# Sparse attention and a Fourier mixing block on one core: the first attention in program order without weight conversion beside it, one mask pattern, block sums by pair, and seven products for eight in half of the first second layer

## The chip, the cores and the metric

The kernel runs on one core of a Trainium2 chip. The metric is the device time of one execution in microseconds (us). Five engines work side by side: TensorE (PE in the profile; its weight loads are PEld), VectorE (DVE), ScalarE (ACT), GpSimd (POOL) and SyncE (SP), which here only issues DMAs. SBUF holds tiles of 128 partitions, PSUM holds what TensorE sums up.

## What is computed

The reference has two parts, all in f32.

```python
# attention: q, k, v are (4, 8, 768, 64)
k_sum = k.reshape(B, H, nb, block, D).max(axis=3)      # block = 32, nb = 24
v_sum = v.reshape(B, H, nb, block, D).mean(axis=3)
mask_l = np.abs(pos[:, None] - pos[None, :]) < window  # window = 16
scores_all = concat([where(mask_l, scale * q @ k.T, -1e9), scale * q @ k_sum.T + log(block)])
attn = softmax(scores_all) @ concat([v, v_sum])
# mixing: x is attn as (4, 768, 512); w_ch1 (512, 2048) and w_ch2 (2048, 512) are float64
u = x + real(fft(fft(x, axis=1), axis=2))
un = (u - mean(u)) / sqrt(var(u) + 1e-6)
out = u + max(un @ w_ch1, 0) @ w_ch2
```

Each query thus sees the keys at a distance under 16 and one summary of each block of 32 keys: the maximum of the keys, the mean of the values, with 32 in the weight. The batch has four images.

## The kernel before, in words

All the work is in `_main_program`. The four images pass one after another through attention, a Fourier stage, a first layer (512 to 2048) and a second layer (2048 to 512), the two layers in two halves c = 0, 1 of eight blocks j of hidden columns: `gen_hidden(b, 0)`, `gen_out(b, 0)`, `gen_hidden(b, 1)`, `gen_out(b, 1)`. Attention of image b + 1 is mixed into the layers of image b, and the last `gen_out` of an image is mixed with the Fourier stage of the next one.

**First attention (image 0).** Heads are taken in four pairs g. `load` fetches q and k of a pair (`qn`, `kn`, 384 KB each). `prepare` (L656) transposes them by products with the identity (L668), ScalarE copies them into `qt` and `kt` (L670), and VectorE takes the maxima of blocks (`km`, L679). `wide_scores` (L685) goes over 12 windows of 64 queries and 96 keys (L695), with 32 rows more for the block maxima (L699); ScalarE takes the exponential (L701) and VectorE multiplies by the mask `wide`, one pattern of 64 columns for each of the 12 windows, because the first and last window have keys outside the sequence. `wide_values` (L713) multiplies by the values `vw` (L718), whose 65th column holds `count` and so gives the divisor, and VectorE divides (L723 and a multiplication). `block_sums` (L584) fetches the values once more, for two pairs together (four loads `vb`, 96 rows of 512), and adds them up on GpSimd (L563), for image 1 on VectorE (L560 and L605). `sum_values` (L705) picks a pair's sums by a product with `sel` (L709) and ScalarE spreads them into rows 96 to 128 of `vw` (L710). Images 1 to 3 use narrower windows (`scores`, `sum_scores`, `values`).

**Weights.** `w_ch1` and `w_ch2` arrive as 64-bit words. `convert` (L847) turns half a block into f32: four VectorE operations of 128x512 (L857, L858, L862, L864), two on ScalarE (L859, L860) and a multiplication. `make` (L870) does so for both halves of a block, forms the sums that the seven products of W1 need, and stores the block to DRAM (`dw1`, `dw2`) for the later images. `plan` (L827) lists the blocks with the stage that must have been issued before each: `(1, 0, None)` is W1's first block, done during the first attention, `(1, 1, ("fold", 0))` the second, after the fold of image 0. For image 1 `get_w2` (L915) fetches four parts of a W2 block, forms the other three (`_right_sums`, four VectorE subtractions of 128x256), and stores them.

**Fourier stage.** `gen_fourier` (L972) folds `x` on VectorE (sums and differences of halves, with three small copies in each of two rounds), TensorE multiplies by tables along the sequence (`y`, L1014) and along the columns (`mx`, L1040 for image 0, L963 later), VectorE adds and normalizes, TensorE transposes (`unt`, L1079). `keep_busy` (L952) issues products without use while image 0 is folded.

**Layers.** `gen_hidden` (L1086) forms each 2x2 of blocks by seven products for eight (L1101); ScalarE and VectorE combine them (L1111 and after). `gen_out` (L1133) is plain for image 0: 6 row tiles, 4 blocks, 2 halves, each product with 512 columns (L1142), then one addition to `x` for each tile. For later images it takes three pairs of row tiles, and in each seven products, summed over four blocks, of 256 columns (L1167); four left sums of 128x512 go before, and seven additions of 128x256 to `x` come after.

**Order.** SP issues the DMAs of `fetch` in program order up to the layers of image 0, over eight DMA semaphores in rotation, so that a DMA waits for the landing of the eighth before it. The other engines are ordered by the scheduler of the Tile framework, by its own estimate of times and by priorities (`drive`, L1243, raises them for the first of its generators). PSUM has four buffers for attention (`abank`) and four for the rest (`bank`).

Of the kernel before, what the change touches and what calls it, by code (L numbers as in the profile page):

```python
# [16 lines left out]
P = 128  # L17
# [405 lines left out]
def _tables(S, DM):  # L423

    g = _general_consts(S, DM)
    nb = S // BLOCK

    r, i, c = np.arange(96)[:, None, None], np.arange(S // QB)[None, :, None], np.arange(QB)[None, None, :]
    tok = QB * i - W + r
    wide = np.ones((P, S // QB, QB), dtype=np.float32)  # L430
    wide[0:96] = (r > c) & (r < c + 2 * W) & (tok >= 0) & (tok < S)
    count = np.zeros((P, 1), dtype=np.float32)
    count[0:96], count[96:96 + nb] = 1.0, BLOCK

    r, i, c = np.arange(64)[:, None, None], np.arange(nb)[None, :, None], np.arange(BLOCK)[None, None, :]
    tok = BLOCK * i - W + r
    near = (r > c) & (r < c + 2 * W) & (tok >= 0) & (tok < S)
    near = np.concatenate([near, near]).astype(np.float32)


    sel = np.zeros((4 * nb, 2, 2, 2, 32), dtype=np.float32)
    half = np.zeros((2, 2, 32, 2), dtype=np.float32)
    for h in range(2):
        half[:, h, :nb, h] = 1.0
        for e in range(2):
            for pair in range(2):
                for n in range(nb):
                    sel[(2 * pair + e) * nb + n, pair, e ^ h, h, n] = 1.0

    fs = np.ascontiguousarray(np.moveaxis(g["fs"], 2, 0))  # L450


    fd = g["fd"].reshape(P, 6, DM // 2)
    n = DM // 4
    odd = fd[:, 1, 1:n].copy()
    odd[0] = 0.0
    fm = np.concatenate([fd[:, 0, 0:n + 1], fd[:, 3, 0:n], odd, fd[:, 4, 0:n], fd[:, 1, 0:n + 1]], axis=1)
    fm = np.ascontiguousarray(fm)
    return dict(wide=wide, near=near, sel=sel.reshape(4 * nb, 2, P), half=half.reshape(P, 2), count=count, fs=fs,
                fd=g["fd"], fm=fm, ident=g["ident"])  # L460
# [26 lines left out]
def _main_program(ctx, tc, q, k, v, moe_w_ch1, moe_w_ch2, out):  # L487
# [36 lines left out]
    wide = bpool.tile([P, NC, 2, S], FP, tag="h", name="wide").rearrange("p j h s -> p (j h s)")  # L524
    wide = wide[:, 0:NQ * QB].rearrange("p (n c) -> p n c", n=NQ)
    near = cpool.tile([P, 2, NB2, BLOCK], FP, name="near")
    sel = cpool.tile([4 * nb, 2, P], FP, name="sel")
    half_of = cpool.tile([P, 2], FP, name="half")
    count = cpool.tile([P, 1], FP, name="count")
    rebias = cpool.tile([P, 1], FP, name="rebias")  # L530
# [52 lines left out]

    def block_sums(b, gg):  # L584

        f = BLOCK // 4
        n = f * D
        if done_weights:
            raw = room(f"vb_{b}_{gg}")
            raw = [raw[0:4 * nb, n * i:n * (i + 1)] for i in range(4)]  # L590
        else:

            raw = [bpool.tile([P, NC, P], FP, tag="s", bufs=5, name=f"vb_{b}_{gg}_{i}").rearrange("p n t -> p (n t)")
                   [0:4 * nb] for i in range(4)]
        for i in range(4):
            fetch(out=raw[i], in_=v[b, 4 * gg:4 * gg + 4].rearrange("h (n f) d -> (h n) (f d)", f=BLOCK)
                  [:, n * i:n * (i + 1)])
        vb = spool.tile([4 * nb, D], FP, tag="vbs", bufs=2, name=f"vbs_{b}_{gg}")

        add = tt if b == 1 else gtt  # L600
        add(raw[0], raw[0], raw[1], ADD)
        add(raw[2], raw[2], raw[3], ADD)
        add(raw[0], raw[0], raw[2], ADD)
        if b == 1:
            nc.vector.tensor_reduce(out=vb, in_=raw[0].rearrange("p (f d) -> p d f", d=D), op=ADD, axis=AX.X)  # L605
        else:
            while f > 2:
                f //= 2
                gtt(raw[0][:, 0:f * D], raw[0][:, 0:f * D], raw[0][:, f * D:2 * f * D], ADD)
            gtt(vb, raw[0][:, 0:D], raw[0][:, D:2 * D], ADD)  # L610
        sums[b, gg] = vb

# [7 lines left out]
    def load_values(b, g):  # L620
        if g % 2 and following(b, g, 1):
            block_sums(*divmod((b * NP + g + 1) // 2, NP // 2))
        (load_wide_values if is_wide(b) else load_narrow_values)(b, g)

    def load_wide_values(b, g):

        vw = wide_vw(g)
        for e in range(2):
            off = v[b, 2 * g + e].offset
            parts = [(W, WK, 0, NQ), (0, W, 1, NQ)] if (b, g, e) == (0, 0, 0) else [(0, WK, 0, NQ)]  # L630
            for r0, r1, i0, i1 in parts:
# [4 lines left out]
    def load_narrow_values(b, g):  # L636
# [3 lines left out]
        if g < 2 and is_wide(b - 1):  # L640
            nc.gpsimd.memset(vw[WK:P, :, D:D1], 1.0)
        for e in range(2):
# [12 lines left out]

    def prepare(b, g):  # L656
        qn, kn = nat[b, g]
        kt, km = kt_bufs[g % 2], km_bufs[g % 2]
        qt = apool.tile([P, S], FP, tag="qt", name=f"qt_{b}_{g}")
        for src, dst in ((kn, kt[:, W:W + S]), (qn, qt)):  # L660
            if is_wide(b):
                for j0, j1 in ((0, 2), (2, 3)):
# [22 lines left out]
    def wide_scores(b, g):  # L685
# [3 lines left out]
        for half in range(2):  # L689
# [10 lines left out]
            for e in range(2):  # L700
                nc.scalar.activation(out=p[:, e, n0:n1], in_=ps[e], func=AF.Exp, scale=SC)  # L701
                tt(p[:, e, n0:n1], p[:, e, n0:n1], wide[:, n0:n1], ALU.mult)
        return p

    def sum_values(b, g):  # L705

        ps = abank([P, 2, D], f"vs_{b}_{g}")
        for e in range(2):
            nc.tensor.matmul(ps[WK:P, e], sel[:, g % 2, D * e:D * e + 32], sums[b, g // 2], start=True, stop=True)  # L709
        nc.scalar.copy(out=wide_vw(g)[WK:P, :, :, 0:D],  # L710
# [43 lines left out]
    def values(b, g, p, pm, x):  # L754
        vw = vw_bufs[g % 2]
        ps = abank([P, D], f"vs_{b}_{g}")
        nc.tensor.matmul(ps, sel[:, g % 2, :], sums[b, g // 2], start=True, stop=True)
        tt(vs[:, :, 0:D], ps[:, None, :].to_broadcast([P, 2, D]),
# [29 lines left out]
    def gen_attention(b):  # L788
        x = bpool.tile([P, NST, DM], FP, tag="x", bufs=2, name=f"x_{b}")
        x_of[b] = x  # L790
        for g in range(NP):
            p = (wide_scores if is_wide(b) else scores)(b, g)
            yield
            if is_wide(b):
                sum_values(b, g)
            else:
                sum_scores(b, g, p[1])
            n1, n2 = following(b, g, 1), following(b, g, 2)
# [3 lines left out]
            if n1:  # L802
                with tc.issue_after(marks["last av"]) if early else ExitStack():
                    prepare(*n1)

# [5 lines left out]
            if not early:  # L811
                if is_wide(b):
                    wide_values(b, g, p, x)
                else:
                    values(b, g, *p, x)
            if n2:
                load_values(*n2)
            if (b, g) == (0, 0):
                load_raw(2)
            yield  # L820
# [5 lines left out]

    plan = [(1, 0, None), (1, 1, ("fold", 0)), (1, 2, ("mx", 0)), (2, 0, ("mx", 0)), (1, 3, ("h", 0, 0)), (2, 1, ("mx", 0)),  # L827
            (2, 2, ("mx", 0)), (2, 3, ("mx", 0)), (1, 4, ("h", 0, 1)), (1, 5, ("h", 0, 2)), (1, 6, ("h", 0, 3)),
# [41 lines left out]
    def make(f, j):  # L870
# [10 lines left out]
        if f == 1:  # L881
            _left_sums(tt, lambda i: wv[:, i])
        else:

            to, wv = to[:, 0:4], wv[:, 0:4]
        yield
        stores.append((to, wv))
# [27 lines left out]
    def get_w2(b, j):  # L915
# [3 lines left out]
        wt[2, b, j] = w  # L919
        if b == 1:  # L920
            fetch(out=w[:, 0:4], in_=dw2[j][:, 0:4])
# [50 lines left out]
    def gen_fourier(b):  # L972
# [10 lines left out]
        for par in range(2):  # L983
# [5 lines left out]
            keep_busy(b, par, zw)  # L989
            nc.vector.tensor_copy(out=zq[:, par], in_=zw[:, :, Q])  # L990
            nc.vector.memset(fg[:, :, Q:Q + 1], 0.0)
            tt(fg[:, :, 1:Q], zw[:, :, 1:Q], zw[:, :, HD - 1:Q:-1], ADD)
            tt(fg[:, :, Q + 1:HD], zw[:, :, 1:Q], zw[:, :, HD - 1:Q:-1], SUB)
            nc.vector.tensor_copy(out=fg[:, :, 0:DM:HD], in_=zw[:, :, 0:DM:HD])
            tt(fg[:, :, HD + 1:HD + Q], zw[:, :, HD + 1:HD + Q], zw[:, :, DM - 1:HD + Q:-1], SUB)
            tt(fg[:, :, HD + Q:DM - 1], zw[:, :, HD + 1:HD + Q], zw[:, :, DM - 1:HD + Q:-1], ADD)
            ins = nc.vector.tensor_copy(out=fg[:, :, DM - 1:DM], in_=zw[:, :, HD + Q:HD + Q + 1])
            fgs.append(fg)
# [134 lines left out]
    def gen_out(b, c):  # L1133
        x, h = x_of[b], wt["h", b]
        js = range(NC * c, NC * (c + 1))
        if b == 0:

            for t in range(NST):
# [7 lines left out]
                tt(x[:, t, :], ps, x[:, t, :], ADD)  # L1146
                if NC * (c + 1) == NJ:
                    fetch(out=out[b, P * t:P * (t + 1), :], in_=x[:, t, :])
            issued.add(("o", b, c))
# [46 lines left out]
    load(0, 0)  # L1196
    fetch(out=wide, in_=dr["wide"].ap())
    nc.scalar.dma_start(out=count, in_=dr["count"].ap())
# [3 lines left out]
    for kt, km in zip(kt_bufs, km_bufs):  # L1202
        nc.vector.memset(kt[:, 0:W], 0.0)
        nc.vector.memset(kt[:, W + S:], 0.0)
        nc.vector.memset(km, 0.0)
    nc.vector.memset(vw_bufs[0][0:W, 0, 0:D], 0.0)
    block_sums(0, 0)
    load_values(0, 0)
    load(0, 1)
    prepare(0, 0)  # L1210
    for vw in vw_bufs:
        nc.gpsimd.tensor_copy(out=vw[:, :, D], in_=count.to_broadcast([P, nb]))
    load_values(0, 1)
# [26 lines left out]
    attn, weights = gen_attention(0), gen_weights()  # L1240
    drive((first(attn, 6), 1, 0))
    with tc.issue_after(marks["av", 0, 1]):
# [4 lines left out]
    fetch(out=near, in_=dr["near"].ap().rearrange("p (h i) c -> p h i c", h=2))  # L1247
    drive((attn, 1, 600), (first(weights, 18), 3, 0))
    attn = gen_attention(1)
    drive((gen_fourier(0), 4, 600), (first(weights, 66), 12, 0), (first(attn, 5), 1, 0))  # L1250
    for b in range(B):

# [66 lines left out]
```

## Time and profile before

| | |
|---|---|
| median of 4 runs | 849.03 us (848.49 to 849.54) |
| the profiled execution | 849.31 us |
| its span | 847.5 us, so 1.8 us lie around it |
| TensorE busy | 813.9 us, 96% of the span |
| VectorE busy | 479.7 us, 57% |
| ScalarE, GpSimd busy | 230.2 us, 27%; 36.9 us, 4% |
| granted TensorE clock, mean | 0.987 of full speed |
| DMA | 120.94 MB, mean 143 GB/s |

The stages of image 0 lie, by the lines that run, at about 0 to 56 (attention), 56 to 105 (Fourier), 105 to 163 (hidden, first half), 163 to 205 (out, first half, beside hidden work), 205 to 242 (hidden, second half) and 242 to 305.5 (out, second half, with the Fourier stage of image 1).

How to read it: a group of instructions has a line, an engine, an operation and the tiles (out<-in), the number of instructions, their busy time and mean duration, and the idle time of the engine before them with what ended it. One f32 product appears as two records, so `x192` of L1142 are 96 products. "PEclk" is the clock that TensorE was granted, as a share of the full one. A DMA share near or above 1 is read as full DMA engines. The chain of waits follows the work that ended last back through what released it.

### The profile page before, as it was taken

The page shows a single profiled execution, that of the slowest core. Times are in us where ns is not written, and L with a number is a line of the kernel's source. Part 1 is how long each engine was busy: PE and PEld are TensorE (multiplying, and loading weights), DVE is VectorE, ACT ScalarE, POOL GpSimd, SP SyncE. Part 2 cuts the span into 40 slices and gives each one's busy share as a digit, 9 for nine tenths or more (in the row PEclk, how much of TensorE's full clock was granted, in tenths as well). Part 3 has the DMA queues.
Part 4 walks back from the last instruction along what each step waited for, and adds up shares of the span by engine and source line. Part 5 has one row for each costly group of instructions (what it writes and reads, how often), then busy time and mean ns, then how long its engine had stood idle before and what let it go on. Part 6 is the DMA issues. An engine that isn't in the chain of part 4 may idle for free.

```text
span 847.5 us, 14497 instructions
## 1 busy us (share of the span) xinstructions
PE 813.9 (96%) x6006; PEld 568.9 (67%) x6006; DVE 479.7 (57%) x1115; ACT 230.2 (27%) x473; POOL 36.9 (4%) x44
## 2 busy tenths in 40 slices
PE   5979998999999999999999999999999999999997
PEld 4857755545557555787667875688667885786586
DVE  2487996986976543544447943443338953532352
ACT  3524666552621113122232103220321112101100
POOL 3200002003000200001000000000000000000000
PEclk8969999999999999999999999999999999999999
DMA  9998685979523273453933236403411326205001
GB/s 213 229 279 159 150 240 184 263 241 300 200 81 131 75 266 133 124 112 146 250 101 102 74 117 232 106 25 78 174 60 57 113 61 249 87 1 217 1 27 53
DMA packets 102858, 120.94 MB, mean 143 GB/s; under 512 B 50592, under 2 KB 83584, under 8 KB 102784
## 3 DMA queue, kind: packets, MB, share of 16 engines
q1 hardware_dynamic: 102240, 119.77, 48.4%
q8 instruction: 49, 0.80, 0.4%
q10 hardware_dynamic: 544, 0.17, 0.1%
q14 instruction: 25, 0.20, 0.1%
HBM read 95.80 MB, written 24.12 MB: 141 GB/s over the span
## 4 chain that ended last, share of the span: by engine, by line
PE 79%; DVE 9%; ACT 5%; DMA 4%; issue 1%; SPq 1%; ACTq 0%; DVEq 0%
PE hx L1101 18%; PE ox L1167 13%; PE o L1142 9%; PE hz L1101 9%; PE oz L1167 7%; PE hy L1101 4%; PE y L1014 3%; PE oy L1167 3%; DVE x L560 2%; PE sc L735 2%; PE mx L963 1%; ACT qt L678 1%; ACT kt L678 1%; PE sc L695 1%; DMA kn<-in_k_dram 1%
## 5 line engine op out<-in xcount | busy, mean ns | idle before, releaser
L1101 PE MATMUL hx<-u,w 128*128 128x384 f32 x512 | 186.1, 492 | 8.4 <-ACT h L1111 6.1
L1101 PEld LDWEIGHTS hx<-u,w 128*128 128x128 f32 x512 | 94.4, 190 | 75.0 <-ACT h L1111 9.4
L1101 PE MATMUL hz<-u,w 128*128 128x384 f32 x256 | 93.2, 486 | 0.0
L1142 PE MATMUL o<-w,h 128*128 128x512 f32 x192 | 84.9, 595 | 0.0
L1101 PEld LDWEIGHTS hz<-u,w 128*128 128x128 f32 x256 | 48.6, 190 | 33.9 <-ACT h L1118 0.2
L1167 PE MATMUL ox<-w,s 128*128 128x256 f32 x288 | 69.0, 381 | 0.4 <-DVE x L560 0.3
L1167 PE MATMUL oz<-w,s 128*128 128x256 f32 x288 | 68.7, 379 | 0.0
L1167 PE MATMUL ox<-w,h 128*128 128x256 f32 x288 | 66.9, 380 | 0.0
L1142 PEld LDWEIGHTS o<-w,h 128*128 128x128 f32 x192 | 35.7, 190 | 41.9 <-issue 39.9
L560 DVE TENSOR_TENSOR x<-ox,x 128x256 f32<-128x256 f32 x72 | 30.2, 421 | 55.8 <-PE ox L1167 55.8
L1167 PEld LDWEIGHTS ox<-w,h 128*128 128x128 f32 x288 | 54.4, 190 | 8.3
L1167 PEld LDWEIGHTS ox<-w,s 128*128 128x128 f32 x288 | 53.9, 190 | 8.4 <-DVE x L560 1.2
L1167 PEld LDWEIGHTS oz<-w,s 128*128 128x128 f32 x288 | 54.4, 190 | 7.2
L560 DVE TENSOR_TENSOR h<-hx,h 128x384 f32<-128x384 f32 x32 | 17.8, 557 | 71.4 <-PE hx L1101 71.4
L560 DVE TENSOR_TENSOR h<-hy,h 128x384 f32<-128x384 f32 x32 | 17.8, 557 | 57.2 <-PE hy L1101 54.1
L1111 ACT COPY h<-hx 128x384 f32<-128x384 f32 x32 | 15.3, 477 | 121.7 <-PE hx L1101 110.0
L1101 PE MATMUL hy<-u,w 128*128 128x384 f32 x128 | 46.5, 486 | 0.0
L679 DVE TENSOR_REDUCE km<-kt 128x24 f32<-128x768 f32 x16 | 15.2, 951 | 38.9 <-ACT kt L678 24.8
L1127 ACT ACTIVATE h<-hx 128x384 f32<-128x384 f32 x32 | 15.7, 490 | 79.2 <-PE hx L1101 79.2
L1014 PE MATMUL y<-fs,fold 128*128 128x193 f32 x192 | 37.1, 336 | 0.0
L1014 PEld LDWEIGHTS y<-fs,fold 128*128 128x128 f32 x192 | 31.1, 189 | 7.5 <-issue 6.3
L1101 PEld LDWEIGHTS hy<-u,w 128*128 128x128 f32 x128 | 24.3, 190 | 17.0
(125 smaller groups left out, 1104.3 us busy)
## 6 DMA issues: line engine op xcount, KB each, us to landing
w<-dw SPq DMA_DIRECT2D x40, 896.0 KB, 5.2
words<-in_moe_w_ch_dram SPq DMA_DIRECT2D x32, 512.0 KB, 6.5
vw<-in_v_dram SPq DMA_DIRECT2D x47, 192.0 KB, 5.8
dw<-w SPq DMA_DIRECT2D x8, 896.0 KB, 7.2
kn<-in_k_dram SPq DMA_DIRECT2D x16, 384.0 KB, 4.6
qn<-in_q_dram SPq DMA_DIRECT2D x16, 384.0 KB, 5.3
vb<-in_v_dram SPq DMA_DIRECT2D x32, 192.0 KB, 5.6
out_dram<-x SPq DMA_DIRECT2D x24, 256.0 KB, 2.4
```

The costliest lines, as they stand in the source:

```text
L560: nc.vector.tensor_tensor(out=out, in0=in0, in1=in1, op=op)
L678: nc.scalar.copy(out=dst[D * e:D * (e + 1), s:S:2], in_=ps[D * s:D * (s + 1)])
L679: nc.vector.tensor_reduce(out=km[:, 0:nb], in_=kt[:, W:W + S].rearrange("p (n f) -> p n f", f=BLOCK), op=ALU.max, axis=AX.X)
L695: nc.tensor.matmul(ps[e][0:WK, n - n0, :], kt[rows, QB * n:QB * n + WK], qt[rows, QB * n:QB * (n + 1)], start=True, stop=True)
L735: nc.tensor.matmul(ps[h][r:r + 64, i, :], kt[rows, o:o + 64], qt[rows, o:o + BLOCK], start=True, stop=True)
L963: nc.tensor.matmul(out, y[:, g], table, start=True, stop=last, skip_group_check=True)
L1014: nc.tensor.matmul(y, fgs[par][:, st, P * g:P * (g + 1)], fs[par][:, g % 2, st, :], start=(st == 0), stop=(st == HT - 1))
L1101: nc.tensor.matmul(ps, w[:, a, kk, :], u[:, r, kk, :], start=start and kk == 0, stop=stop and kk == 1, skip_group_check=True)
L1111: nc.scalar.copy(out=c11, in_=X)
L1127: nc.scalar.activation(out=c21, in_=X, func=AF.Relu)
L1142: nc.tensor.matmul(ps, h[:, n, hf, P * t:P * (t + 1)], wt[2, b, j][:, 2 * hf:2 * hf + 2, :], start=(n, hf) == (0, 0), stop=(n, hf) == (NC ...
L1167: nc.tensor.matmul(ps, left[a][:, n, :], wt[2, b, j][:, r, :], start=start and n == 0, stop=stop and n == NC - 1, skip_group_check=True)
```

## The change

1. TensorE is issued in program order in both stretches that hold the first attention. The block sums' product of pair 0 moves between the transposes of k and of q of pair 1.
2. No weight is converted during the first attention: W1's first block waits for the fold, its second for the mixing (`mx`). The raw words are fetched before the values of the pair after next.
3. The mask `wide` has one pattern of 64 columns (33 KB for 393 KB, on ScalarE's queue). The keys outside the sequence are left out by zeroes in `vw` and in `count`, which is now a table for each window. Each head's values arrive in three loads: the first window, the ten in the middle, the last.
4. Block sums of the first two pairs are made for each pair (48 rows, two chains on GpSimd). Those of image 1's first two pairs move from VectorE to GpSimd, and those of its other two pairs to after the Fourier stage of image 0.
5. Two products of zeroes, 128x512, run at the very start, after a GpSimd memset.
6. The fold's small copies move from VectorE to ScalarE, for all images.
7. The second half of image 0's second layer uses seven products for eight; the first half stays plain. For W2's blocks 4 to 7 `make` forms the right sums, with all seven parts stored, and image 1 forms them only for blocks 0 to 3.

The core of the diff:

```diff
-    wide = np.ones((P, S // QB, QB), dtype=np.float32)
-    wide[0:96] = (r > c) & (r < c + 2 * W) & (tok >= 0) & (tok < S)
+    wide = np.ones((P, QB), dtype=np.float32)
+    wide[0:96] = (r > c) & (r < c + 2 * W)
+    count = np.zeros((P, S // QB), dtype=np.float32)
+    count[0:96] = (QB * i - W + r >= 0) & (QB * i - W + r < S)
+    count[96:96 + nb] = BLOCK
...
-    def block_sums(b, gg):
+    def block_sums(b, gg, g=None):
+        rows, heads = (4 * nb, slice(4 * gg, 4 * gg + 4)) if g is None else (2 * nb, slice(2 * g, 2 * g + 2))
...
-        add = tt if b == 1 else gtt
+        add = tt if (b, gg) == (1, 1) else gtt
...
-        if g % 2 and following(b, g, 1):
+        if g % 2 and following(b, g, 1) and (b, g) != (1, 1):
             block_sums(*divmod((b * NP + g + 1) // 2, NP // 2))
...
-            parts = [(W, WK, 0, NQ), (0, W, 1, NQ)] if (b, g, e) == (0, 0, 0) else [(0, WK, 0, NQ)]
+            parts = [(W, WK, 0, 1), (0, WK, 1, NQ - 1), (0, WK - W, NQ - 1, NQ)]
...
-                tt(p[:, e, n0:n1], p[:, e, n0:n1], wide[:, n0:n1], ALU.mult)
+                tt(p[:, e, n0:n1], p[:, e, n0:n1], wide[:, None, :].to_broadcast([P, NQ // 2, QB]), ALU.mult)
...
-    plan = [(1, 0, None), (1, 1, ("fold", 0)), (1, 2, ("mx", 0)), (2, 0, ("mx", 0)), (1, 3, ("h", 0, 0)), (2, 1, ("mx", 0)),
+    plan = [(1, 0, ("fold", 0)), (1, 1, ("mx", 0)), (1, 2, ("mx", 0)), (2, 0, ("mx", 0)), (1, 3, ("h", 0, 0)), (2, 1, ("mx", 0)),
...
+        elif j < NC:
+
+            to, wv = to[:, 0:4], wv[:, 0:4]
         else:
-
-            to, wv = to[:, 0:4], wv[:, 0:4]
+            _right_sums(tt, lambda i: wv[:, i])
...
-        if b == 1:
+        if b == 1 and j < NC:
             fetch(out=w[:, 0:4], in_=dw2[j][:, 0:4])
...
-            nc.vector.tensor_copy(out=zq[:, par], in_=zw[:, :, Q])
+            nc.scalar.copy(out=zq[:, par], in_=zw[:, :, Q])
...
-        if b == 0:
+        if (b, c) == (0, 0):
...
+    zeros = bpool.tile([P, 7, 2, S2], FP, tag="u", name="zeros").rearrange("p a k n -> p (a k n)")[:, 0:640]
+    nc.gpsimd.memset(zeros, 0.0)
+    ps = bank([P, 512], "warm")
+    for i in range(2):
+        nc.tensor.matmul(ps, zeros[:, 512:640], zeros[:, 0:512], start=True, stop=True)
...
-    block_sums(0, 0)
+    block_sums(0, 0, 0)
     load_values(0, 0)
     load(0, 1)
+    block_sums(0, 0, 1)
...
-    drive((first(attn, 6), 1, 0))
+    with tc.manual_schedule(engines={mybir.EngineType.PE}):
+        drive((first(attn, 6), 1, 0))
...
-    drive((attn, 1, 600), (first(weights, 18), 3, 0))
+    with tc.manual_schedule(engines={mybir.EngineType.PE}):
+        drive((attn, 1, 600), (first(weights, 18), 3, 0))
     attn = gen_attention(1)
     drive((gen_fourier(0), 4, 600), (first(weights, 66), 12, 0), (first(attn, 5), 1, 0))
+    block_sums(1, 1)
```

The pair 2 and 3 sums of image 0 are still made for both pairs together, behind the loads of pair 1's values. By the instruction order of the built kernel TensorE's value products of pair 1 and scores of pair 2 still stand in alternation, as before; the other steps of the first attention stand one behind the other.

## The prediction

> **What bounds the kernel now.** I read the totals and the slices of the page first, then the windows cut at the stages, then the chain of waits, then the groups of the stages that the change touches.
>
> ```profile
> span 847.5 us, 14497 instructions
> PE 813.9 (96%) x6006; PEld 568.9 (67%) x6006; DVE 479.7 (57%) x1115; ACT 230.2 (27%) x473; POOL 36.9 (4%) x44
> PE   5979998999999999999999999999999999999997
> DVE  2487996986976543544447943443338953532352
> DMA  9998685979523273453933236403411326205001
> ```
>
> TensorE is the bound for the whole kernel, but slices 1 to 8 (21 us each) show two rivals: the DMA engines are full in the first three, and VectorE is at 7 to 9 tenths from the third to the eighth. The windows say how far each stage is from full (columns: stretch, its length, busy time and count of PE, PEld, DVE, ACT, POOL, granted clock, DMA share, GB/s):
>
> ```profile
> 16.00:36.00 20.00, 17.47 (x263) 14.58 (x265) 7.00 (x14) 8.92 (x16) 6.46 (x8) 0.84 1.10 236
> 36.00:56.00 20.00, 19.06 (x261) 14.41 (x259) 13.95 (x33) 9.89 (x16) 0.27 (x2) 0.85 1.04 297
> 82.00:105.00 23.00, 21.31 (x387) 17.37 (x386) 22.05 (x68) 12.45 (x24) 0.00 (x0) 1.00 0.65 156
> 105.00:163.00 58.00, 53.49 (x460) 30.09 (x460) 47.94 (x94) 36.62 (x70) 6.36 (x6) 1.00 0.80 235
> 205.00:242.00 37.00, 36.96 (x115) 21.44 (x114) 24.73 (x50) 20.39 (x39) 0.00 (x0) 1.00 0.62 204
> 242.00:305.50 63.50, 63.50 (x242) 36.67 (x241) 37.80 (x103) 8.71 (x23) 5.27 (x5) 1.00 0.29 99
> ```
>
> The first two rows are the first attention: transfers wait for the DMA engines (share over 1) and TensorE's clock is cut. From 82 to 163 us VectorE is nearly as full as TensorE. From 205 us TensorE has no gap, so only fewer matmuls help there. The chain shows what the start and the end of the first attention hang on (start, duration, what):
>
> ```profile
> 9.19 9.67 DMA kn<-in_k_dram
> 19.00 4.54 PE qk L668 x48
> ...
> 52.65 1.03 DVE p L560 x2
> 53.67 0.60 DVE vb L560
> 54.27 0.15 DVE rec L723
> 54.42 0.93 DVE vbs L605
> 55.35 0.46 DVE x L560
> 55.81 0.60 DVE words L862
> 56.41 0.10 DVE rec L723
> 56.52 0.57 DVE words L864
> 57.08 0.47 DVE x L560
> 57.55 0.60 DVE w L560
> 58.15 1.68 DVE fold L560
> ```
>
> The last value product ends at 55.47, and the fold starts 2.60 later (58.07 in the timeline) because block sums (vb, vbs) and a conversion (words, w) sit on VectorE between the two divisions.
>
> **Half Strassen in the first second layer.** Removed are 6 tiles x 4 x 2 = 48 products of 512 columns, added 3 x 7 x 4 = 84 of 256. An f32 product is two records.
>
> ```profile
> 284.06 21.46 PE o L1142 x50
> L1142 PE MATMUL o<-w,h 128*128 128x512 f32 x96 | 42.0, 592 | 0.0
> L560 DVE TENSOR_TENSOR x<-o,x 128x512 f32<-128x512 f32 x5 | 3.4, 685 | 8.9 <-PE o L1142 8.9
> ```
>
> The chain has 50 records in 21.46 us, 0.429 each, so 96 cost 41.2; 168 of half the columns, at 0.215, cost 36.0. The stage is 63.50 of 63.50 full, so up to 5.2 us leave the path. VectorE gets 12 left sums of 128x512 (about 0.6, 7.2) and 21 output additions (0.34 to 0.42, 7.1 to 8.8) for 6 plain ones (3.6 to 4.1): 10 to 13 more on 37.8 of 63.5. It still fits, but the fold and the norm of image 1 share that engine; I allow 1.2 of TensorE waits (bounds 0 and 5.2): **-4.0**. The 16 right sums of the second four W2 blocks (0.418 each, 6.7) come out of image 1's hidden stage into 205 to 242, where VectorE is idle 12.3 of 37: nothing, or up to 6.7 if they land where it is full. Stored and fetched bytes are equal.
>
> **First attention.** Before qk of pair 2 in SP's order stood 18 loads and stand now 28: six value loads a pair for two or three, sums by pair, less the table of 393 KB (33 KB now, on ScalarE's queue). 360 KB at the window's 236 GB/s are 1.5 us; ten more issues at 0.3 to 0.45 are 3 to 4.5. kn of pair 2, landing at 26.64 before, lands by that between 25.1 and 31.1. Behind the table's place, kn of pair 1 (18.86) comes at 14 to 15, and the two idle stretches of TensorE before 19 us (3.54 for the block sums, 1.04 for kn) go: a pair's sums need half the loads and their additions have 48 rows (between half and all of the 1.26 that 96x512 takes), and the sum product now has the transposes ahead of it. What is late next is kn of pair 2, with TensorE in order behind it: I take qk of pair 2 at 28.0 (29.11 before). SP also waits for GpSimd's additions before it may overwrite the second pair's rows, and the value loads and kn queue behind that wait; that is in my 31.1. From qk of pair 2 to the last value product it took 26.4. The same work at the rows' full-clock durations is 20.2: two qk of 3.0, two scores of 4.15, three value products of 1.62, two sums. So the attention ends between 48.2 and 54.4; nothing tells which end is nearer, since the loads of pair 3 remain and the clock may be cut again; the middle is 51.3: **-4.2** (-7.3 to -1.1). The page's clock is half at 15.7 to 22.5 and at 49.8 to 63.5, and at 32 to 55 TensorE has no gap over 0.35 us. So a gap doesn't explain the second cut, and density of small products may bring it again.
>
> [...]
>
> [...]
>
> **From the value product to the fold.** No block sums and no conversion stand there now: 1.3 (two divisions, as 0.15 + 0.46 twice, and latency) for 2.6: **-1.3** (bounds -1.5 and 0).
>
> **After the fold.** The conversion of W1's first block moves from the attention to here. By the groups of 105 to 163 a half block costs VectorE (5.4 + 5.0 + 8.9 + 9.3 + 8.3) / 12 = 3.08, a block 6.15. Off VectorE come the (1,0) block sums, 2.7 (to GpSimd, idle then), later the (1,1) sums return there. VectorE waits some 6.4 us for TensorE's y products; that hides one block, and pushes the next toward the hidden layer. I take **0** for the whole; bounds: -2 (score products done earlier) and +6.15.
>
> **The rest.** The small copies to ScalarE take 6 x 0.16 off VectorE in each fold, 0 to -1 us; the mask's broadcast has the same elements (1.16 per two). Two zero products at the start could save the 2 us by which the first transposes (2.83 + 2.2) exceed later ones (1.53 + 1.48), hidden because kn of pair 1 comes later: 0 (bounds -2 and +0.9). Images 1 to 3 keep their matmuls: 0.
>
> **Sum.** -4.0 - 4.2 - 1.3 = -9.5 on the profiled 849.31 (span 847.5 and 1.8 around it): **839.8**. The median shown is 849.03, 0.3 less, inside its own scatter.
>
> **Rivals.** (1) *The attention stays bound by transfers*: kn of pair 2 at 31, the later loads pushed as far, no gain of 4.2: 844.0. For it speak DMA shares of 1.04 to 1.10; against it, fewer bytes. (2) *VectorE becomes the bound after the fold*: one block unhidden, +6.15: 846.0. For it speak 22.05 of 23 busy. (3) *Slower, by the same engine with everything exposed*: the conversion (6.15) and the right sums (6.7) both stand in TensorE's way between the fold and 242, +12.85 on 839.8: 852.7. It loses from 9.5 + 1.7 = 11.2 unhidden on; against it speak the 12.3 idle at 205 to 242. (4) *It doesn't do what it says*: half Strassen's gain is lost to left sums that wait for VectorE: 843.8. (5) *Better*: attention at 48.2 (-7.3), Strassen -5.2, fold -1.5, copies -1: 834.3.
>
> **How the numbers follow.** Forecast (838 to 842) 0.46, better 0.10, (1) 0.15, (4) 0.08, (2) 0.12, (3) 0.09. A measurement of this kernel can tell about 0.2%, 1.7 us, from no change. Rival (2) gives two thirds of its chance to faster and a third (0.04) to the same, where a little more of a second block shows. Faster: 0.46 + 0.10 + 0.15 + 0.08 + 0.08 = 0.87; same 0.04; slower 0.09. The range from better to rival (2), **834.0 to 846.0**, leaves out the 0.13 and some edges.
>
> **What will show it.** The groups of the second layer: o 96 records for 192, each of ox, oz 336 for 288 or near; the stage of 63.5 near 59.5. The last value product near 51 and the fold 1.3 behind; qk of pair 2 near 28, released by a DMA. VectorE waits in TensorE's gaps of the first hidden stage: 4 to 5 us is right, 10 is rival (2). Wrong it would be if the granted clock stays half through more of the first 60 us, or if SP waits for GpSimd beyond 31 us.

## The result, and the profile after

The changed kernel takes 850.15 us (median of 52 runs) beside 848.3 for the kernel before (77 runs): ratio 1.0022, 95% interval 1.0014 to 1.0030. That is 1.9 us slower, where 839.8 was forecast. The profiled execution took 848.85 us with a span of 846.7, 1.3 under its median, while that of before lay 1.0 over its own; so the two traces end nearly level (spans of 847.5 and 846.7), and they are used for where time went, not for the sum.

The windows of the kernel after, cut like those of before:

```profile
16.00:36.00 20.00, 13.01 (x212) 11.29 (x207) 6.48 (x10) 7.73 (x13) 10.65 (x12) 0.83 0.84 199
36.00:56.00 20.00, 17.90 (x310) 13.81 (x308) 8.56 (x20) 8.60 (x16) 6.01 (x7) 0.98 1.09 291
105.00:163.00 58.00, 51.70 (x438) 30.16 (x437) 51.61 (x101) 33.87 (x66) 7.07 (x6) 0.94 0.85 244
205.00:242.00 37.00, 36.59 (x214) 21.53 (x214) 30.96 (x69) 21.10 (x40) 0.57 (x1) 1.00 0.76 244
242.00:305.50 63.50, 62.97 (x327) 52.61 (x326) 50.18 (x128) 11.12 (x32) 5.39 (x5) 1.00 0.26 94
```

In the first row TensorE falls from 17.47 to 13.01 busy, and the DMA engines from 1.10 to 0.84: neither of the two engines that had been full is so any more, and something else holds both. GpSimd rises from 6.46 to 10.65. In the third row VectorE rises from 47.94 to 51.61 and TensorE falls. The chain of waits of the kernel after names what holds the first stretch:

```profile
11.42 6.89 DMA vb<-in_v_dram
...
18.45 1.28 POOL vb L563
...
19.74 0.31 SPq L547
...
20.10 6.38 DMA words<-in_moe_w_ch_dram
...
26.50 1.05 SPq L547
...
27.65 3.82 DMA kn<-in_k_dram
31.61 3.87 PE qk L672 x40
...
54.80 1.16 PE av L723 x20
...
57.30 1.77 DVE fold L560
```

The rows for pair 1's sums land, GpSimd's addition of them releases SP, and behind that stand the loads up to kn of pair 2. SP's own waits from 10 to 32 us:

```profile
SPq L547 <- POOL vb L563: 3.4, 5, 1.4
SPq L547 <- DMA vb<-in_v_dram: 3.3, 1, 3.3
SPq L547 <- POOL vbs L563: 1.1, 1, 1.1
SPq L547 <- DMA words<-in_moe_w_ch_dram: 0.9, 1, 0.9
```

The first three, 7.8 us in all, are waits for buffers of the sums: for GpSimd's additions, and for the landing of the rows that they add up. Before, the same waits for GpSimd were 1.4, and kn of pair 2 was issued once TensorE had freed its buffer, at 23.1. The fourth is another thing: one load of weight words (512 KB), which in the program stands behind k and q of pairs 2 and 3, was issued at 20.10 among the sums' rows, so here SP did not keep the program's order throughout, and the last value load ahead of kn waited for its landing at 26.48. It is not what made kn late: in e8 below no such load was issued before 30, and kn of pair 2 landed at 31.57.

Kn of pair 2 lands at 31.47 (26.64 before), and TensorE idles 6.56 us ahead of its transposes. The account by stages, from the first and last TensorE records of each:

| stretch | before | after | forecast | measured |
|---|---|---|---|---|
| start to the last value product | 55.5 | 56.1 | -4.2 | +0.7 |
| TensorE idle until the fold's products | 4.4 | 3.0 | -1.3 | -1.4 |
| from there to the first hidden product | 45.1 | 44.3 | 0 | -0.8 |
| first hidden half and first half of the second layer | 100.5 | 106.4 | 0 | +5.9 |
| second hidden half | 36.6 | 36.6 | 0 | 0 |
| second half of the second layer | 63.3 | 59.1 | -4.0 | -4.2 |
| image 1's first hidden half | 45.7 | 47.1 | 0 | +1.4 |
| from there to the last product | 490.3 | 488.8 | 0 | -1.5 |

The measured column adds up to 0.1; behind the last product the trace of after is 0.8 shorter. Half Strassen did what was forecast in its stage, as the groups of 242 to 305.5 show:

```profile
L1174 PE MATMUL ox<-w,s 128*128 128x256 f32 x48 | 11.7, 379 | 0.0
L560 DVE TENSOR_TENSOR x<-ox,x 128x256 f32<-128x256 f32 x11 | 4.6, 418 | 2.8 <-PE ox L1174 2.8
```

TensorE waits for nothing there. What it gained was lost at the start and between 105 and 210. The timeline of the kernel after shows a part of the second loss (start, duration, engine, line; in brackets the idle time before):

```profile
131.10 1.75 POOL L563 TENSOR_TENSOR vb_None<-vb_None,vb_None 96x512 f32<-96x512 f32 x1 [74.76 <-DMA vb_None<-in_v_dram]
133.41 1.49 DVE L864 TENSOR_SCALAR words<-words 128x512 int32<-128x512 int32 x1
134.82 1.76 DVE L560 TENSOR_TENSOR w<-words 128x512 f32<-128x512 f32 x1
140.83 1.65 PE L1110 MATMUL hx<-u,w 128*128 128x384 f32 x2 [2.70 <-DVE h L560]
```

Conversion of weights fills VectorE, operations of 0.42 and 0.68 (at 127.66 and 138.96, with no addition on GpSimd) take 1.49 and 1.76 beside GpSimd's additions, an addition for the hidden layer stands behind them, and TensorE waits 2.70. That wait is a small part of the +5.9. The two stretches from the first hidden product to the second hidden half, before and after:

```profile
105.00:205.50 100.50, 94.79 (x772) 50.57 (x771) 85.48 (x168) 53.42 (x99) 13.35 (x12) 1.00 0.84 242
103.40:209.80 106.40, 99.71 (x773) 53.78 (x772) 93.40 (x185) 54.04 (x101) 13.55 (x12) 0.97 0.85 249
```

VectorE is busy 7.9 longer, but TensorE stands idle only 1.0 longer (6.7 for 5.7). The score products of image 1 take 1.6 longer (192 records in 5.0 us for 3.4), and the clock is half for 6.8 us (from 126.8 and from 140.4, 3.4 each) for none. Four hx records took 2.77 at 127.09 and take 1.45 at 145.00; by that those 6.8 us cost, as an estimate, at most 3.4.

### The profile page after: what moved, and what is told of

Same layout as the page of the kernel before. It is cut to its first block, busy times and chain, and to the rows that moved or that the text cites. A ratio compares the mean times of both kernels' runs of the same rounds, so it can differ in the third digit from the quotient of the medians.

```text
span 846.7 us, 14736 instructions
## 1 busy us (share of the span) xinstructions
PE 810.7 (96%) x6082; PEld 582.2 (69%) x6082; DVE 488.9 (58%) x1117; ACT 232.8 (27%) x497; POOL 48.4 (6%) x57
## 4 chain that ended last, share of the span: by engine, by line
PE 82%; DVE 7%; ACT 5%; DMA 3%; issue 1%; SPq 1%; ACTq 0%; POOL 0%; POOLq 0%
PE hx L1110 19%; PE ox L1174 16%; PE hz L1110 9%; PE oz L1174 8%; PE o L1151 5%; PE hy L1110 4%; PE oy L1174 4%; PE y L1023 4%; PE sc L740 2%; DVE x L560 2%; PE mx L971 2%; ACT kt L682 1%; ACT qt L682 1%; PE qk L680 1%; PE av L773 1%; PE unt L1088 1%
## 5 line engine op out<-in xcount | busy, mean ns | idle before, releaser
L1110 PE MATMUL hx<-u,w 128*128 128x384 f32 x512 | 189.2, 497 | 8.6 <-DVE h L560 3.8
L1174 PE MATMUL ox<-w,s 128*128 128x256 f32 x336 | 80.7, 381 | 0.3
L1174 PE MATMUL oz<-w,s 128*128 128x256 f32 x336 | 80.5, 379 | 0.0
L1174 PE MATMUL ox<-w,h 128*128 128x256 f32 x336 | 78.0, 380 | 0.0
L560 DVE TENSOR_TENSOR x<-ox,x 128x256 f32<-128x256 f32 x84 | 35.2, 421 | 60.9 <-PE ox L1174 60.8
L1174 PEld LDWEIGHTS ox<-w,h 128*128 128x128 f32 x336 | 63.4, 190 | 9.7
L1174 PEld LDWEIGHTS ox<-w,s 128*128 128x128 f32 x336 | 62.8, 190 | 9.4 <-DVE x L560 1.1
L1174 PEld LDWEIGHTS oz<-w,s 128*128 128x128 f32 x336 | 63.5, 190 | 8.4
L560 DVE TENSOR_TENSOR h<-hx,h 128x384 f32<-128x384 f32 x32 | 17.8, 555 | 67.4 <-PE hx L1110 67.4
L560 DVE TENSOR_TENSOR h<-hy,h 128x384 f32<-128x384 f32 x32 | 17.8, 556 | 59.7 <-PE hy L1110 56.5
L1110 PE MATMUL hy<-u,w 128*128 128x384 f32 x128 | 46.5, 486 | 0.0
L1151 PE MATMUL o<-w,h 128*128 128x512 f32 x96 | 42.4, 596 | 0.0
L1174 PE MATMUL oy<-w,h 128*128 128x256 f32 x168 | 39.7, 379 | 0.0
L1023 PEld LDWEIGHTS y<-fs,fold 128*128 128x128 f32 x192 | 31.1, 189 | 7.7 <-issue 5.1
```

Source lines behind the costliest of these rows:

```text
L560: nc.vector.tensor_tensor(out=out, in0=in0, in1=in1, op=op)
L1023: nc.tensor.matmul(y, fgs[par][:, st, P * g:P * (g + 1)], fs[par][:, g % 2, st, :], start=(st == 0), stop=(st == HT - 1))
L1110: nc.tensor.matmul(ps, w[:, a, kk, :], u[:, r, kk, :], start=start and kk == 0, stop=stop and kk == 1, skip_group_check=True)
L1151: nc.tensor.matmul(ps, h[:, n, hf, P * t:P * (t + 1)], wt[2, b, j][:, 2 * hf:2 * hf + 2, :], start=(n, hf) == (0, 0), stop=(n, hf) == (NC ...
L1174: nc.tensor.matmul(ps, left[a][:, n, :], wt[2, b, j][:, r, :], start=start and n == 0, stop=stop and n == NC - 1, skip_group_check=True)
```

## The experiments

Each ratio is to the kernel before, run beside it, with a 95% interval; a difference between two kernels is that of their ratios times 848.3.

**e1, e2: half Strassen alone on the kernel before, and taken out of the kernel after.**

```diff
-        if b == 0:
+        if (b, c) == (0, 0):
...
-        if b == 1:
+        if b == 1 and j < NC:
```

(with the right sums of blocks 4 to 7 in `make`; e2 is the reverse of it.)

> The kernel before with half Strassen alone (the second half of image 0's second layer by seven products, W2's blocks 4 to 7 stored with their right sums). Theory A (half Strassen is worth what its matmuls say; the change lost its gain elsewhere): the stage from 242 us shrinks from 63.5 to 59 or 60, no other stage grows by more than 0.5, total -3.5 to -4.5 against before, ratio 0.995 to 0.996. Rival B (half Strassen's VectorE work, 12 left sums, 21 additions and 16 right sums, costs as much in its neighbours as it saves): ratio 0.999 to 1.001, with new TensorE waits on VectorE between 163 and 242 or in image 1's first hidden half.

> The kernel after with the second layer of image 0 plain in both halves again. Theory A: +4 against after, ratio to before 1.006 to 1.008, and all of the difference between 246 and 305 us. Rival B: no slower than after, ratio to before 1.001 to 1.003.

e1: 847.09, ratio 0.9992 (0.9974 to 1.0011). e2: 853.47, ratio 1.0060 (1.0041 to 1.0079). In e1 the stage fell from 63.3 to 59.3, as theory A had it, but image 1's first hidden half grew from 45.7 to 47.9, which neither theory named (B had put new waits there among others). In e2 that half is 45.7 again and the stage 63.3. So half Strassen is worth 4.0 to 4.2 where it runs and gives 1.4 to 2.2 back in the next stage. In the kernel after it is worth 3.2 by e2's ratio. In the kernel before e1 shows 0.7 and, by its interval, at most 2.2, which includes the 1.8 that its stages add up to; by its ratio e1 lies in rival B's range, not in theory A's.

**e3: the loads that TensorE needs first go ahead of the sums' rows.**

```diff
     def load_values(b, g):
+        if (b, g) == (0, 1):
+            load(0, 2)
+            load_wide_values(b, g)
         if g % 2 and following(b, g, 1) and (b, g) != (1, 1):
             block_sums(*divmod((b * NP + g + 1) // 2, NP // 2))
-        (load_wide_values if is_wide(b) else load_narrow_values)(b, g)
+        if (b, g) != (0, 1):
+            (load_wide_values if is_wide(b) else load_narrow_values)(b, g)
...
     load_values(0, 1)
-    load(0, 2)
```

> The kernel after with one change of SP's order: k and q of pair 2 and the values of pair 1 are fetched ahead of the rows for the block sums of pairs 2 and 3, whose buffers GpSimd has yet to free. Theory A (the attention's gain was lost because SP stood behind GpSimd's additions, so that kn of pair 2 landed at 31.5 and TensorE idled 6.6 us): kn of pair 2 lands at 21 to 25, the idle stretch ahead of its transposes falls under 1.5 us, the last value product ends at 51 to 53.5 instead of 56.1, total -2.5 to -4.5 against after. Rival C (the attention is bound by the DMA engines as a whole, and whatever is loaded earlier makes the rest later): kn of pair 2 is early, but the wait returns at the values or at pair 3; the last value product ends at 55 to 56.5 and the total stays within 1 of after.

843.75, ratio 0.9951 (0.9929 to 0.9973): 6.0 better than after. The chain of waits of e3:

```profile
27.16 2.85 PE qk L676 x48
...
48.16 2.92 PE av L727 x45
```

Pair 2's transposes follow at 27.16 on the products before them, with no DMA between, and the last value product ends at 51.1. Theory A holds, with 6.0 where it gave at most 4.5; the DMA engines were not the bound (rival C).

**e4: the plan of conversions of before, in the kernel after.**

```diff
-    plan = [(1, 0, ("fold", 0)), (1, 1, ("mx", 0)),
+    plan = [(1, 0, None), (1, 1, ("fold", 0)),
```

> The kernel after with the plan of conversions of before: W1's first block during the first attention, the second from the fold on. Theory D (the first hidden half of image 0, 56.9 us instead of 51.5, grew because a block's conversion of 6.15 us on VectorE was pushed into it): hidden goes back to 51 to 53.5, the attention and the fold end at most 1.5 later, total -2.5 to -5 against after. Rival E (the hidden half grew because of the image 1 block sums there, beside GpSimd's additions, and two cuts of the clock, not for the conversion): hidden stays at 55.5 or more, the total within 1.2 of after.

844.65, ratio 0.9957 (0.9936 to 0.9977): 5.5 better than after. The first hidden half took 46.5, the stretch to the end of the first second-layer half 98.8 for 106.4; the fold's products began 1.4 later. Theory D holds, with a larger gain than it gave. The cuts of the clock that after has at 126.8 and 140.4 are absent, but they are not needed for the loss: e3, which keeps the new plan, has none between 58.3 and 839.9. From the fold's products to the second hidden half it is 143.0 to 148.6 us in all nine kernels whose plan converts W1's first block during the attention, and 150.1 to 151.9 in all seven that convert it after the fold.

**e5: both of these.** The edits of e3 and e4 together.

> The kernel after with both edits of the two runs before: loads of pairs 2 and 1 ahead of the second sums, and W1's first block converted in the first attention again. Theory A with D (two independent losses: SP behind GpSimd, and a block's conversion in the first hidden half): the gains add up, 6.4 and 5.5 off 850.2 give 838 to 840; fold at 54 to 56, first hidden half 46 to 48. Rival F (they share one cover: a shorter attention has no room for a conversion, which then delays the masks on VectorE or the loads): 842 to 844, with the last value product at 53 or later.

851.68, ratio 1.0036 (1.0020 to 1.0052). Two edits that gained 6.0 and 5.5 gained nothing together (1.2 slower than after, with intervals that overlap). The timeline of e5:

```profile
40.70 4.73 POOL L563 TENSOR_TENSOR vb_None<-vb_None,vb_None 96x512 f32<-96x512 f32 x3
41.16 1.49 DVE L868 TENSOR_SCALAR words<-words 128x512 int32<-128x512 int32 x1
42.57 1.75 DVE L560 TENSOR_TENSOR w<-words 128x512 f32<-128x512 f32 x1
50.53 2.62 PE L703 MATMUL sc<-qt,kt 64*96 64x64 f32 x24 [8.08 <-DVE x L560]
```

The conversion stands on VectorE ahead of pair 2's division and runs beside GpSimd's block sums; TensorE waits 8.08 us for the PSUM buffer that the division frees. In e4 kn of pair 2 came late: the conversion began at 37.36 and pair 2's value products ended only at 49.27, so the division waited 0.6 for what was left of it. In e5 it began at 37.68, those products ended at 40.52, and the division started at 49.61. The two edits share that cover, as rival F says, but its 842 to 844 is missed by 8.

**e6: image 1's W2 fetch and right sums issued at the end of the hidden block** (on e5; `get_w2(b, j)` moved behind the block's products for b = 1).

> The same as the run above, and image 1's fetch and right sums of each W2 block are issued at the end of its hidden block instead of at its start. Theory G (half Strassen gives 1.1 to 2.0 back in the next stage: its products hold the W2 buffers to the end, so image 1's W2 blocks land later and VectorE waits for them ahead of the first hidden additions): the gap of 1 to 2 us some 9 us into image 1's first hidden half goes, total -1 to -2 against the run above. Rival H (the gap has another cause, or the waiting sums then fall late in front of the second layer): total within 0.7 of the run above or slower.

850.57, ratio 1.0024 (1.0008 to 1.0039). Inconclusive: the scheduler set the right sums ahead of the hidden additions all the same, and the wait stayed at 1.49.

**e7: the new plan alone, on the kernel before** (the reverse of e4's lines).

> The kernel before with one change: no conversion in the first attention (W1's first block after the fold, the second after mx). Theory D (the plan alone costs the first hidden half a block's conversion): the attention ends up to 1 earlier and the fold starts up to 2 earlier, the stretch from the first hidden product to the end of the first second-layer half grows from 100.6 to 104.5 to 108, total +2 to +6 against before. Rival E (the plan is harmless by itself; only together with the sums moved beside it does it cost): total -2 to +1.

854.39, ratio 1.0065 (1.0043 to 1.0087). The stretch of the two first halves grew from 100.5 to 104.4, near the 104.5 that theory D gave at least. The attention got 3.2 longer in the trace, against it: its half-rate stretch lay at 44.3 to 57.9 instead of 49.8 to 63.5, so wholly inside the attention. That execution lay 3.4 over its median.

**e8: the kernel after without the fixed order** (both `manual_schedule` lines out).

> The kernel after without the fixed order of TensorE in the first attention. Theory A (TensorE has nothing else to do while kn of pair 2 is missing, since the order of the scheduler before was nearly the same): the idle stretch before pair 2's transposes stays at 5 to 7, total within 1.5 of after. Rival I (the fixed order is what makes TensorE wait): the stretch shrinks by 2 or more, the attention ends at 54 or earlier, total -2 or more against after.

854.85, ratio 1.0081 (1.0054 to 1.0108): 5.0 slower than after. The wait for kn of pair 2 stayed (5.92), but theory A's "within 1.5" fell, and so did rival I. A window of e8:

```profile
50.00:64.00 14.00, 13.68 (x102) 9.18 (x102) 4.05 (x8) 3.66 (x6) 4.31 (x6) 0.52 1.16 310
```

And a window of the kernel after, of the same length:

```profile
36.00:50.00 14.00, 13.66 (x238) 10.62 (x237) 5.71 (x15) 5.55 (x12) 3.29 (x4) 1.00 1.11 252
```

TensorE is busy for 13.7 of 14 us in both, with 102 records at half the clock in one and 238 in the other. From the fold on the two traces take equally long (150.7 to the second hidden half), so the loss is in the attention, whose last value product ends at 64.9 for 56.1; its trace lies 2.8 over its median, that of after 1.3 under its own. The order makes a difference also at the granted clock of 1.00, which the kernel before has in both of these rows:

```profile
24.91 1.24 PE L695 MATMUL sc<-qt,kt 64*96 64x64 f32 x24
42.99 1.23 PE L695 MATMUL sc<-qt,kt 64*96 64x64 f32 x12
```

In the first row the records of the two heads of a pair start 6 to 7 ns apart, and the next two 85 ns after them; in the second the scheduler has set one head's products behind the other's, single records start every 85 ns, and half as many take as long.

**e10: e5 with image 1's first block sums on VectorE.**

```diff
-        add = tt if (b, gg) == (1, 1) else gtt
+        add = tt if b == 1 else gtt
```

> The kernel with loads first and the old plan (e5, 851.7), and image 1's first block sums on VectorE as in the kernel before, not on GpSimd. Theory L (e5 lost what each edit had won because the conversion on VectorE ran beside GpSimd's additions and took 1.2 to 1.75 an operation instead of 0.42 to 0.68, with pair 2's division queued behind it, so that TensorE waited 8.1 for its PSUM buffer): the operations go back to 0.42 to 0.68, the wait falls to 3 to 5, total 846 to 849. Rival M (only the order on VectorE counts: the conversion stands ahead of the division): the wait stays at 7 or more, total within 1.5 of 851.7.

848.71, ratio 1.0002 (0.9983 to 1.0021). The timeline of e10:

```profile
43.08 0.44 DVE L868 TENSOR_SCALAR words<-words 128x512 int32<-128x512 int32 x1
48.61 2.61 PE L703 MATMUL sc<-qt,kt 64*96 64x64 f32 x24 [4.23 <-DVE x L560]
```

Theory L holds: 1.49 is 0.44 again, and the wait is 4.23 for 8.08. The half that is left is put down to the place ahead of the division; e15 below differs from e10 in that place alone and is 6.5 faster.

**e11, e12: the order alone on the kernel before, and the order with half Strassen** (the two `manual_schedule` lines; in e12 also e1's edit).

> The kernel before with one change: TensorE in program order in the two stretches of the first attention. Theory J (program order keeps the products dense, so that the cut of the clock from 49.8 to 63.5 us goes, as it is absent in the ordered kernels where nothing stops TensorE for long): no half-rate stretch of 13.7 us, or one of 3.4 to 6.8 from a gap, the last value product at 50 to 53 instead of 55.5, total -2 to -5 against before. Rival K (the order makes TensorE wait for masks and divisions that the scheduler's alternation covered): gaps of 2 or more in 30 to 55, total -1 to +3.

> The kernel before with the order of TensorE and half Strassen, and nothing else. If both are worth what theories J and A say, -2 to -5 and -1 to -3: 841 to 846. Rival K: 846 or more, not better than half Strassen alone (847.1).

e11: 847.27, ratio 1.0009 (0.9990 to 1.0028); e12: 846.56, ratio 0.9988 (0.9969 to 1.0006). In e11 the last value product ends at 52.4 and the clock is whole from 23.8 to 54.5, as theory J has it, but TensorE then waits 5.19 for the fold (4.40 before), since block sums and conversion still stand there on VectorE, and 2.92 in the first hidden half. Of the 3.1 that the attention gained, its trace keeps 2.2 at the last product; the total is not to be told from that of before. And e12, whose attention is the same, has the clock cut from 48.9 to 59.2, right after the attention's last wait of 1.69 us (46.8 to 48.5), so the fixed order does not by itself keep the clock: theory J holds for e11's trace alone. With half Strassen, e12 lies just outside the 841 to 846 of both theories together.

**e13: e3 with image 1's first block sums on VectorE** (e10's line on e3).

> The kernel after with loads first (e3, 843.75) and image 1's first block sums on VectorE as before. In e3 three mask products beside GpSimd's additions took 1.05 each for 0.52. Theory L: they go back to 0.55, but VectorE gets 2.7 of sums there: the attention ends within 1.5 of e3's 51.1, total 842.5 to 846. Rival N (moving these sums to GpSimd was what made the change's attention short): the last value product at 53 or later, total 846.5 or more.

844.64, ratio 0.9947 (0.9928 to 0.9967), the attention at 50.5. Moving these sums to GpSimd made no difference that shows (rival N falls).

**e14: e3 with the right sums of all eight blocks in `make`.** The first half of image 0's second layer here multiplies by a part of W2 that the right sums have overwritten, with the same instructions.

```diff
-        elif j < NC:
-
-            to, wv = to[:, 0:4], wv[:, 0:4]
         else:
             _right_sums(tt, lambda i: wv[:, i])
```

> The kernel after with loads first (e3, 843.75), and the right sums of all eight W2 blocks are formed with their conversion, so that image 1 forms none. Theory G (half Strassen gives back 1.1 to 2.0 in image 1's first hidden half because VectorE waits there for W2 blocks that land later, with the first hidden additions queued behind the right sums): the gap of 1.3 before the third block of hidden products goes and that half falls from 47.3 to 45.5 to 46; the 6.7 of right sums for blocks 0 to 3 move to VectorE's fullest stretch, so the time from the first hidden product to the end of the first second-layer half grows from 107.0 by 0 to 6.7. Rival H (that gap has another cause): the half stays at 47 or more.

843.37, ratio 0.9938 (0.9920 to 0.9957). A group of image 1's first hidden half in e3:

```profile
L1114 PE MATMUL hx<-u,w 128*128 128x384 f32 x64 | 23.6, 494 | 2.4 <-DVE h L560 1.3 <-ACT h L1124 1.1
```

The same group in e14:

```profile
L1106 PE MATMUL hx<-u,w 128*128 128x384 f32 x64 | 23.5, 493 | 1.1 <-ACT h L1116 1.1
```

The wait for VectorE is gone and the half takes 45.7 for 47.3. Theory G holds for that half. The total is no better than e3's within the intervals: the two first halves take 108.2 for 107.0 and the second hidden half 37.5 for 36.6. When the blocks are fetched is read from SP in the traces: before, its three fetches of W2 blocks issue from 300.4 on, 5 us ahead of the first hidden product; after, from 304.4 on, with two stores of results between, 1 us ahead. That the plain row tiles leave one block after the other while the seven products hold all four to the end fits this, and was not tried by itself.

**e15: e13 with the first conversion behind pair 2's division**, the second from the fold on.

```diff
-    plan = [(1, 0, ("fold", 0)), (1, 1, ("mx", 0)),
+    plan = [(1, 0, ("av", 0, 2)), (1, 1, ("fold", 0)),
```

(`wide_values` marks `("av", b, g)` as issued.)

> The kernel after with loads first and image 1's first block sums on VectorE (e13, 844.64), and W1's first block is converted behind the division of pair 2, its second from the fold on. Theory P (the block that the plan pushes behind the fold costs 4 to 7 in the first hidden half also in the mended kernel, and VectorE has room for it late in the attention if it does not stand ahead of pair 2's division): no wait of TensorE over 2 between 38 and 50, the fold at most 3 later than 53.3, the stretch from the first hidden product to the end of the first second-layer half 102 to 104 for 108.3, total 840 to 843. Rival Q (the room is not there: what the hidden half wins, the fold loses): total 843.5 to 847.

842.17, ratio 0.9925 (0.9906 to 0.9943): the lowest ratio of all, 8.2 better than after; against e3, e13 and e14 its interval overlaps. No wait over 1.7 between 38 and 50; the fold's products begin 3.6 later than in e13 and the first hidden product 7.1 later, but the two first halves take 98.1 for 108.3. Theory P holds in the stages, with a larger gain and a larger price than it gave; the 1.9 between the totals of e13 and e15 are inside the noise.

## Why the prediction was wrong

**Half Strassen: right in its stage, mis-sized in the sum.** -4.2 was measured for -4.0. The 1.2 of waits I allowed lie elsewhere: not at the fold or the norm, but 1.4 in image 1's first hidden half (e14). So the term is -2.8 in the traces, -3.2 by e2, and less on the kernel before (e1). The right sums of blocks 4 to 7 cost nothing, as priced: the second hidden half is 36.6 in both.

**First attention: the step that failed is "I take qk of pair 2 at 28.0".** It began at 31.61. I priced SP's ten more issues and the bytes, and put SP's wait for GpSimd into the upper bound alone. That wait set the time: SP stood 7.8 us at the sums' buffers, 4.5 of them for GpSimd, kn landed just past the upper bound (31.47 for 31.1), and the DMA engines stood at 0.84. The sign that I named for this, waits of SP for GpSimd beyond 31, is absent: the last of them ends at 22.3, and six value loads and the landing of kn follow. Without that stop e3's attention ends at 51.1, where 51.3 was forecast, but this is partly luck: its kn lands at 20.89 and TensorE, not a DMA, decides that pair 2 starts at 27.16; and 51.3 was the middle of a range of which I could not tell the likelier end. Rival (1) had the place and the size and the wrong cause: the queue, not the transfers.

**After the fold: the step that failed is "I take 0".** The measured +5.9 is near my upper bound, +6.15. I let 6.4 us of VectorE's idle time before the y products' results hide a block. The trace of before does not have them: from 57 to 82.7 us VectorE is idle for 4.2 in all, 2.5 of them waiting for products. And the plan moves two blocks on by one stage each, so that the hidden half, with VectorE 47.94 of 58 busy, takes what is pushed out. e4 and e15 take it back: 98.8 and 98.1 for 106.4. How it costs there I had wrong too: I looked for waits of TensorE for VectorE, 10 us for rival (2), and there are 2.7; the rest is in spread score products and in the cut clock. That the plan costs this time is shown by its edits; that a fuller VectorE spreads the score products and brings the cuts is my estimate and was not shown (e3, with the new plan, has no cut there).

**Right:** from the value product to the fold -1.4 for -1.3; the later folds, without three small copies, give most of the -1.5 of the rest, a little more than the bound of -1: the two stages that hold them take 59.2 to 59.3 each in every kernel with this edit, 59.8 to 60.0 in every one without.

**The chances.** Rivals (1) and (2) were priced as alternatives, each leaving the other terms as they were. They are two places and both came about: 839.8 + 4.9 + 5.9 = 850.6, of which the other stages give back 1.2; the sum was built on the profiled execution, and that of after took 848.85. One of the two would have left the forecast in its range.

Also open: what the split of the value loads, the smaller mask and the two zero products are worth by themselves was not tried.

## What to carry to other kernels

Here SP stood 7.8 us at buffers of the sums, 4.5 of them for GpSimd, and kn of pair 2, behind them, landed at 31.47; with kn ahead (e3) pair 2 began at 27.16 for 31.61. So put what the bound engine needs next ahead of loads whose buffers a slow engine has yet to free, and price a new chain on a slow engine by the queue that it stops. Work that is taken off one stage is not gone: follow it to the stage that receives it, and if that stage's engine is nearly full, count it in full. Two edits that each win may have used the same idle time, and losses in different places add, so price rivals together as well as one by one.

## What the runs showed of the hardware

In the kernel after the granted clock is 0.50 from 27.8 to 34.6, and TensorE waits 6.56 us up to 31.61 for kn of pair 2. The clock was cut also where TensorE had no gap: before, from 46.40 to 49.80, TensorE is busy for 3.40 us of 3.40 at the clock of 1.00, with 37 product records, and from 49.8 to 63.5 the clock is 0.50. In the kernel after the stretch from 46.50 to 49.90 is as full, with 79 records, and the clock stays at 1.00 up to 55.1. In kernels in program order TensorE waits 1.69 us for the copy of the sums ahead of pair 3's value products. Behind that wait the clock is cut in after (the products start at 53.69, the clock is 0.50 from 55.1 to 62.0) and in e12 (from 48.9 to 59.2); in e11, whose attention is the same as e12's, it is whole up to 54.5. That the density of small products decides, as I supposed in the prediction, fits the stretches at 46.4 and 46.5; what sets a cut off was not shown. By its total the fixed order was worth 5.0 us to the kernel after (e8), a gain that the prediction didn't count, hidden under the two losses; how much of it is the clock and how much the overlap of two heads was not separated, and on the kernel before it did not show (e11).

In e5, beside GpSimd's additions from 40.70 on, four kinds of VectorE operations on 128x512 got longer: L868, with a single input, takes 1.49 (0.42 at 39.28), L872 1.75 (0.68 at 39.61), L874 1.21 (0.69 at 40.55) and the w of L560 1.75. In e10, with those additions on VectorE, they take 0.44, 0.70, 0.70 and 0.70.
